# A dense first stage of seven-product blocks: two of its products made ahead for all chunks by a second level of seven products, through DRAM

## The chip, the cores and the metric

The kernel runs on one core of one Trainium2 chip. The metric is the device time of one execution in microseconds. A profile of one execution stands beside the times; its span runs from the first to the last instruction.

## The reference, cut to what matters

x has 2048 tokens of 640 numbers. The output mixes a Fourier layer and a dense layer with a gate per token:

```
g = sigmoid((x * gate_w).sum(-1))
a = x @ Wd_re.T ;  b = x @ Wd_im.T            # hidden transform, 640 x 640
y = Ws_re @ a - Ws_im @ b                      # sequence transform, 2048 x 2048
h = x @ w1 + b1                                # 640 -> 1728: the "dense first stage"
act = h * tanh(softplus(h))                    # Mish
out = g * y + (1 - g) * (act @ w2)             # 1728 -> 640
```

All in fp32, on the given drawn inputs.

## The kernel before, in words

**Precision.** TensorE works on fp32r. Each operand is split in a high and a low part (`split`, L84: ScalarE copies f to the high part, L82; VectorE subtracts it to make the low part, L79), and `mm3` (L93) makes three matmuls: high x high, high x low, low x high. A matmul has a 128 x 128 stationary weight block and 512 moving tokens. All matmuls are issued at L91.

**Stages.** Sequence transform, hidden transform, dense first stage, last stage, in this order. Tokens are moved in four groups of 512, t = 0 to 3, and a pair tp holds t1 = 2 tp and t2 = 2 tp + 1. Each stage does its matrix product with one level of a scheme of seven products in place of eight: the weights are seen as 2 x 2 blocks, so are the inputs, sums of blocks are multiplied, and the results are added up.

**The dense first stage** (`dense_first`, L766). w1 has 1728 columns: 13 chunks of 128 and a rest of 64. The first 12 chunks are worked as pairs f and f + 6 (six pairs, FP = 6), for each tp. x's 640 rows are five blocks of 128: 0 and 1 are the first half, 2 and 3 the second half, and the fifth one (d) is added as an ordinary product. The moving operands for one tp are a11, a12, a22 (blocks as they are), s1 to s4 (sums of blocks), and d1, d2; each but d has two blocks (k = 0, 1). The products of a pair of chunks are, in order: p1 (weights x a11, into bank a), p5 (x s1, bank b), d (x d2, bank d), p6 (x s2, added in bank a), p3 (x s4 and d1, bank b), p7 (x s3, bank a), p2 (x a12 and d1, bank c), p4 (x a22 and d2, bank a). p1 and p5 are copied out to SBUF by ScalarE (`snap`, L821) and added by VectorE to banks later (`add`, L828). Two chunk pairs are worked side by side, step by step. Mish is applied by ScalarE (`mish`, L703) and the result is stored to DRAM. Chunk 12 and the rest of 64 columns are done ahead of this, per t, in `dense_rest` (L705).

**x's sums.** In `sums_of` (L772) VectorE makes s1 to s4 from four loaded blocks of x, per tp and k, shortly before they are split.

**Weights.** `w1_job` (L637) makes the sums of w1's blocks and splits them: for each chunk pair three weight slots (a, b, c) and a part of a shared one (T2B).

**The order.** The program is written out as a list of steps; each step issues its matmuls. A planner (from L1060) walks the steps: it loads inputs up to AHEAD = 9 steps before they are prepared (L1076, on SP's queue), prepares a step's operands LEAD = 7 steps ahead (6 in the dense stage), issues stores some steps after the data is made (L1085, SP's queue), runs functions registered for a step (`at`), and then fills in background jobs (weight splits, gate rows, gated y rows) when its own clock of VectorE is behind its clock of TensorE. `need` forces a job that a step cannot do without. Buffers are pools handed out in turn: R (pairs rh, rl for moving operands, NR), FS (512 columns of fp32, NFS), FX (640 columns, NFX), W (weight pairs, NW). `lend` jobs turn a weight slot into an R pair (NL of them). No background jobs run in the steps of `quiet` (L1044).

Of the kernel before, what the change touches and what calls it, by code (L numbers as in the profile page):

```python
# [13 lines left out]
P = 128  # L14
N = 512
# [9 lines left out]
LEAD_D = 6  # L25
AHEAD = 9
SPARE, SPARE_D, SPARE_OUT = 3, 5, 4
SLACK, SLACK_UP = -1.0, 2.5
NR, NFS, NFX, NW, NL = 10, 20, 4, 26, 4
# [18 lines left out]
def fnet_mish_gate(ctx: ExitStack, tc: tile.TileContext, xn, xt, c_re, c_im, wd_re, wd_im,  # L48
# [78 lines left out]
    class Job:  # L127
        def __init__(self, key, work, load=lambda: [], w=0, fx=0, fs=0):
            self.key, self.work, self.load, self.w, self.fx, self.fs = key, work, load, w, fx, fs
# [498 lines left out]
    W1, W2C, T2B, extra = [None] * (FC + 1), {}, [None] * 2, []  # L628
# [7 lines left out]

    def w1_job(f, ga, gb):  # L637
        t = FS.get()
        a, b, c = W.get(), W.get(), W.get()
        if f % KD == 0:  # L640
            T2B[f // KD] = W.get()
# [8 lines left out]
        yield 1  # L650
        split(*part(b, 0, 2 * P), t[:, B2])
        split(*part(c, 0, 2 * P), ga[:, A2])
        yield 1
        split(*part(c, 2 * P, 4 * P), gb[:, A2])
        split(*part(c, 4 * P, 5 * P), t[:, :P])
        split(*part(T2B[f // KD], f % KD * P, f % KD * P + P), t[:, P:2 * P])
        FS.put(t)
        FX.put(ga, gb)
        W1[f] = (a, b, c)
# [24 lines left out]
    def dense_jobs():  # L684
        for _ in range(NL):
            jobs.append(Job("lend", simple(lend), w=1))
        jobs.append(Job("w1c", simple(w1c_job), lambda: [fx_load(w1a[FC - 1])], 1, 1))
        jobs.append(Job("w1r", simple(w1r_job), lambda: [fx_load(w1b, KD * FR)], 1, 1))
        for f in range(FP):
            jobs.append(Job(("w1", f), lambda a, b, f=f: w1_job(f, a, b),  # L690
                            lambda f=f: [fx_load(w1a[f]), fx_load(w1a[f + FP])], 3 + (f % KD == 0), 2))
# [13 lines left out]
    def dense_rest(t, keep, preps, end=False):  # L705
# [17 lines left out]
        def post_c():  # L723
            ps, a = H.pop("c"), FS.get()
            mish(a, ps, FC - 1)
            psum.put(ps)
            store(asc[FC - 1][t], a, a)
# [8 lines left out]
        def post_r():  # L736
# [7 lines left out]
            def then():  # L744
                nc.scalar.activation(a[q], a[q], AF.Mish)
                store(asc[FC][t], a[q], a)
            at(n + 2, then)
            if not keep:
                x_free(*keys)
            elif t % 2:  # L750
                x_free(*[("a21", k, t // 2) for k in range(2)])
# [9 lines left out]
        step(raw, [wait], mms_c, post_c)  # L761
        step([], [], mms_r, post_r)
        attach.append((preps[0], lambda: prep(0, 3)))
        attach.append((preps[1], lambda: prep(3, 5)))

    def dense_first(tp, end, ops):  # L766
# [3 lines left out]
        n0 = len(steps)  # L770

        def sums_of(k):  # L772
            raw = [(("xs", tp, a, k), xt[t, kk])
                   for a, t, kk in ((21, t2, k), (22, t2, k + 2), (11, t1, k), (12, t1, k + 2))]

            def prep():
                a21, a22, a11, a12 = (RAW.pop(r[0]) for r in raw)
                s1 = FS.get()
                tt(s1, a21, a22, OP.add)
                tt(a21, a11, a21, OP.subtract)  # L780
                tt(a22, s1, a11, OP.subtract)
                tt(a12, a12, a22, OP.subtract)
                FS.put(a11)
                XS[k] = {"s1": s1, "s2": a22, "s3": a21, "s4": a12}
            return raw, prep

        def make(name):
            def prep():
                if name[0] == "s":
                    for k in range(2):  # L790
                        x_split((name, k, tp), XS[k].pop(name))
                elif name[0] == "d":
# [6 lines left out]
        def sub(fp, ops, then=()):  # L799

            def mms():
                a, b, c = W1[fp]
                for bank, name, blk, start, stop in ops:
                    if start:
                        H[bank, fp] = psum.get()
                    for k in range(2):
                        mm3(H[bank, fp], *blk(a, b, c, k), *X[name, k, tp], start and k == 0, stop and k == 1)
                for bank, name, w, start, stop in then:
                    if start:
                        H[bank, fp] = psum.get()  # L810
                    mm3(H[bank, fp], *part((a, b)[w], 4 * P, 5 * P), *X[name, 0, tp], start, stop)
            return mms

        def at_cols(which, c0):
            return lambda a, b, c, k: part((a, b, c)[which], c0 + k * P, c0 + k * P + P)

        def t2_at(fp):
            return lambda a, b, c, k: part(c, 4 * P, 5 * P) if k == 0 else \
                part(T2B[fp // KD], fp % KD * P, fp % KD * P + P)
# [7 lines left out]

        def add(bank, name, fp, keep=False):  # L828
            f = KEEP[name, fp] if keep else KEEP.pop((name, fp))
            tt(f, H[bank, fp], f, OP.add)  # L830
            return f
# [12 lines left out]
        def parts(fp):  # L844
# [7 lines left out]
            def p1_post():  # L852
                snap("p1", "a", fp)
                free("a11")

            def p5_post():
                snap("p5", "b", fp)
                free("s1")

# [3 lines left out]

            def p3_post():
                o = add("b", "u2", fp)
# [4 lines left out]
            def p7_post():  # L870
                add("a", "p5", fp, True)
                free("s3")

            def p2_post():
                c11, c22 = add("c", "p1", fp), add("d", "p5", fp)
                pop("c", fp)
                pop("d", fp)
                i = clock["step"]
                at(i + 1, lambda: out_act(fa, t1, c11, c11))
                at(i + 2, lambda: out_act(fb, t2, c22, c22))  # L880
                free("a12", "d1")

            def p4_post():
# [7 lines left out]
                if end:  # L891
                    W.put(*W1[fp])
                    if fp in (KD - 1, FP - 1):
                        W.put(T2B[fp // KD])

            return [
                ([lambda: need(("w1", fp))], sub(fp, [("a", "a11", at_cols(0, 0), True, True)]), p1_post),
                ([], sub(fp, [("b", "s1", at_cols(2, 0), True, True)]), p5_post),
                ([], sub(fp, [], [("d", "d2", 1, True, True)]), None),
                ([], sub(fp, [("a", "s2", t2_at(fp), False, True)]), p6_post),  # L900
                ([], sub(fp, [("b", "s4", at_cols(1, 2 * P), False, False)], [("b", "d1", 1, False, True)]), p3_post),
                ([], sub(fp, [("a", "s3", at_cols(2, 2 * P), False, True)]), p7_post),
                ([], sub(fp, [("c", "a12", at_cols(0, 2 * P), True, False)], [("c", "d1", 0, False, True)]), p2_post),
                ([], sub(fp, [("a", "a22", at_cols(1, 0), False, False)], [("a", "d2", 0, False, True)]), p4_post)]


        for fp in range(0, FP, 2):
            for two in zip(parts(fp), parts(fp + 1)):
                for p in two:
                    step([], *p)  # L910
        for name, i in ops:
            if name[0] == "k":
                raw, prep = sums_of(int(name[1:]))
                steps[i][0].extend(raw)
                attach.append((i, prep))
                continue
            kk = {"a11": (t1, 0), "a12": (t1, 2), "a22": (t2, 2), "d1": (t1, 4), "d2": (t2, 4)}.get(name)
            if name[0] == "d":
                steps[i][0].append((("xd", tp, name), xt[kk]))
            elif kk:  # L920
                steps[i][0].extend((("xo", tp, name, k), xt[kk[0], kk[1] + k]) for k in range(2))
            attach.append((i, make(name)))
# [74 lines left out]
    for k in range(KS):  # L997
        jobs.append(Job(("gate", k), simple(lambda f, k=k: gate_rows(k, f)), lambda k=k: [x_rows(k)], fx=1 + (not k)))
    jobs.append(Job("mish", simple(lambda: nc.scalar.preload_act_table_set("mish"))))
# [27 lines left out]
    for tp in range(2):  # L1027
# [3 lines left out]
    dense_rest(2, False, (nd, nd))  # L1031
    dense_rest(3, False, (nd + 2, nd + 2))
    dense_rest(0, True, (nd + 6, nd + 8))
    dense_rest(1, True, (nd + 8, nd + 10), True)
    n0 = nd + 8
    dense_first(0, False, [("k0", n0 + 2), ("k1", n0 + 2), ("s1", n0 + 3), ("s2", n0 + 4), ("s4", n0 + 6), ("s3", n0 + 7)])
    n0 = len(steps)
    dense_first(1, True, [("a11", n0 - 8), ("k0", n0 - 4), ("k1", n0 - 3), ("s1", n0 - 2), ("d2", n0), ("s2", n0 + 2),
                          ("s4", n0 + 4), ("d1", n0 + 5), ("s3", n0 + 7), ("a12", n0 + 9), ("a22", n0 + 11)])
    for t in (2, 3):  # L1040
        at(n0 - 2, lambda t=t: QX.update({t: fx_load(qsc[t], N)}))
        at(len(steps) + 3, lambda t=t: FX.put(QX.pop(t)))
    narrow.update(range(nd, len(steps)))
    quiet = set(range(nd - 4, nd + 13))  # L1044
# [17 lines left out]
    unwritten = {id(d) for row in usc + asc for d in row}  # L1062
# [97 lines left out]
```

## Time and profile before

| what | value |
|---|---|
| median of the runs shown | 864.03 us (863.54 to 864.53, 2 runs) |
| the profiled execution | 864.04 us |
| its span | 862.3 us |
| TensorE / VectorE / ScalarE busy | 857.9 / 716.7 / 472.0 us |
| matmuls | 3775 |
| transfers | 214.12 MB, mean 248 GB/s |
| granted TensorE clock | 1.000 |

How to read the lines that follow: a row of a group gives the line, the engine, the operation, output<-input, the shape and the count, then busy us in all, mean ns of one, and the idle time of the engine just before them with what ended it. A row of a wait reads "who waited <- for whom: us in all, times, longest". A row of a stretch gives start:end, length, and then busy us and instruction count of TensorE, its weight loads, VectorE, ScalarE and GpSimd, then the granted clock, the share of transfer time in use and GB/s. The sequence stage ends near 396 us, the hidden stage near 519, the dense first stage near 689.

### The profile page before, as it was taken

How to read it: one execution, taken by the hardware profiler on the slowest of the kernel's cores; microseconds unless marked ns; L12 is line 12 of the kernel's file. 1: busy time of each engine (PE TensorE's matmuls, PEld its weight loads, DVE VectorE, ACT ScalarE, POOL GpSimd, SP SyncE). 2: the span in 40 equal slices, each digit the busy share in tenths (PEclk: the TensorE clock that was granted, in tenths of full speed). 3: DMA queues.
4: the chain of work that ended last, by engine and by line, in shares of the span. 5: the costliest groups of instructions: out<-in, count | busy, mean ns of one | idle time of the engine just before them, and what ended most of it. 6: DMA issues, size and time to landing. Idle time of an engine off the chain costs nothing.

```text
span 862.3 us, 12147 instructions
## 1 busy us (share of the span) xinstructions
PE 857.9 (99%) x3775; PEld 710.2 (82%) x3775; DVE 716.7 (83%) x1248; ACT 472.0 (55%) x883; POOL 0.2 (0%) x4
## 2 busy tenths in 40 slices
PE   9999999999999999999999999999999999999998
PEld 7888888888888888888888888888888888888886
DVE  6999987989869668998898896685677869999993
ACT  6756545454654545656667566654645647642442
POOL 0000000000000000000000000000000000000000
PEclk9999999999999999999999999999999999999999
DMA  9976748885868573778677697199784777894952
GB/s 348 323 240 221 245 158 303 299 277 200 287 225 280 175 252 119 248 269 302 234 251 241 238 336 252 56 306 334 252 297 165 254 240 237 281 346 169 357 203 109
DMA packets 116752, 214.12 MB, mean 248 GB/s; under 512 B 13520, under 2 KB 16080, under 8 KB 116688
## 3 DMA queue, kind: packets, MB, share of 16 engines
q1 hardware_dynamic: 116256, 212.71, 72.2%
q10 hardware_dynamic: 432, 0.66, 0.2%
q8 instruction: 29, 0.48, 0.2%
q14 instruction: 35, 0.29, 0.1%
HBM read 168.99 MB, written 44.32 MB: 247 GB/s over the span
## 4 chain that ended last, share of the span: by engine, by line
PE 99%; ACT 0%; issue 0%
PE ps L91 99%; ACT f L82 0%
## 5 line engine op out<-in xcount | busy, mean ns | idle before, releaser
L91 PE MATMUL ps<-rh,wh 128*128 128x512 f32 (+1 forms) x1083 | 420.3, 389 | 0.0
L91 PE MATMUL ps<-rh,wl 128*128 128x512 f32 x1067 | 414.1, 389 | 0.0
L91 PE MATMUL ps<-rl,wh 128*128 128x512 f32 x1061 | 411.9, 389 | 0.0
L82 ACT ACTIVATE rh<-f 128x512 fp32r<-128x512 f32 x416 | 245.9, 625 | 164.4 <-DVE f L79 105.8
L79 DVE TENSOR_TENSOR rl<-f,rh 128x512 fp32r<-128x512 f32 x414 | 269.7, 684 | 55.6 <-ACT rh L82 55.1
L91 PEld LDWEIGHTS ps<-rh,wh 128*128 128x128 f32 x1083 | 203.5, 188 | 42.4 <-ACT wh L82 0.2
L91 PEld LDWEIGHTS ps<-rh,wl 128*128 128x128 f32 x1067 | 200.3, 188 | 41.4
L91 PEld LDWEIGHTS ps<-rl,wh 128*128 128x128 f32 x1061 | 199.4, 188 | 41.3
L79 DVE TENSOR_TENSOR f<-f,f 128x512 f32<-128x512 f32 x309 | 210.9, 688 | 10.9 <-DMA f<-act 2.5
L82 ACT ACTIVATE f<-ps 128x512 f32<-128x512 f32 (+1 forms) x144 | 83.7, 596 | 86.7 <-PE ps L91 79.7
L82 ACT ACTIVATE wh<-f 128x512 fp32r<-128x512 f32 (+3 forms) x170 | 75.4, 482 | 57.8 <-DVE f L79 41.8
L79 DVE TENSOR_TENSOR wl<-f,wh 128x512 fp32r<-128x512 f32 (+3 forms) x170 | 81.2, 509 | 23.2 <-ACT wh L82 23.1
L79 DVE TENSOR_TENSOR f<-ps,f 128x512 f32<-128x512 f32 x89 | 57.6, 683 | 21.0 <-PE ps L91 20.9
L91 PE MATMUL ps<-wh,wh 128*128 128x512 f32 x187 | 72.7, 389 | 0.0
L91 PE MATMUL ps<-wl,wh 128*128 128x512 f32 x187 | 72.7, 389 | 0.0
L91 PE MATMUL ps<-wh,wl 128*128 128x512 f32 x181 | 70.4, 389 | 0.0
L703 ACT ACTIVATE f<-f,b1s 128x512 f32<-128x512 f32 x36 | 24.9, 719 | 41.5 <-DVE f L79 41.5
L91 PEld LDWEIGHTS ps<-wh,wh 128*128 128x128 f32 x187 | 35.1, 188 | 7.3
L91 PEld LDWEIGHTS ps<-wl,wh 128*128 128x128 f32 x187 | 35.1, 188 | 7.3
L91 PEld LDWEIGHTS ps<-wh,wl 128*128 128x128 f32 x181 | 34.0, 188 | 7.0
L79 DVE TENSOR_TENSOR wl<-fx,wh 128x640 fp32r<-128x640 f32 (+3 forms) x47 | 31.3, 679 | 3.6 <-ACT wh L82 3.6
L82 ACT ACTIVATE wh<-fx 128x640 fp32r<-128x640 f32 (+4 forms) x48 | 28.7, 612 | 7.9 <-DMA fx<-in_w1a_dram 4.4
(37 smaller groups left out, 162.7 us busy)
## 6 DMA issues: line engine op xcount, KB each, us to landing
f<-in_c_re_dram SPq DMA_DIRECT2D x128, 256.0 KB, 4.2
f<-in_c_im_dram SPq DMA_DIRECT2D x128, 256.0 KB, 4.3
f<-act SPq DMA_DIRECT2D x93, 256.0 KB, 5.4
f<-u SPq DMA_DIRECT2D x80, 256.0 KB, 4.6
act<-f SPq DMA_DIRECT2D x54, 256.0 KB, 4.0
f<-in_xt_dram SPq DMA_DIRECT2D x44, 256.0 KB, 4.9
u<-f SPq DMA_DIRECT2D x40, 256.0 KB, 3.3
y<-f SPq DMA_DIRECT2D x40, 256.0 KB, 4.6
```

The costliest lines, as they stand in the source:

```text
L79: nc.vector.tensor_tensor(o, a, b, op=op)
L82: nc.scalar.activation(o, a, AF.Copy, scale=scale)
L91: nc.tensor.matmul(ps, a, b, start=start, stop=stop, skip_group_check=True)
L703: nc.scalar.activation(o[rows], src[rows], AF.Mish, bias=b1s[rows, f:f + 1])
```

## The change

1. *Products p1 and p5 for all chunks at once.* For all twelve chunks and both token pairs p1 is one product of a block of w1 (6 chunks x 2 k) with x's a11 (2 k x 2 tp). It is itself cut in 2 x 2 blocks: chunk 2g and 2g + 1, k = 0 and 1, tp = 0 and 1, and made with seven products for each of three groups g (`dense_quads`). p5 is done likewise with the sums s1. The results are stored to DRAM, and in `dense_first` they are loaded again (`part_load`, 12 steps ahead for p1, 9 for p5) and copied by ScalarE into the banks a, b, c, d before the other products are added there (`seed`). Two of p5's results stay in SBUF.
2. *Weights for it*: three `quad_job`s of three weight slots each, held to the end of the prelude. `w1_job` splits less.
3. *The order*: the seven-product steps (q) and the eight steps of `dense_rest` (r) are interleaved as "rqqrqqrqqrq", once for p1, once for p5.
4. *x's sums made early* (`x_sum_jobs`): background jobs behind the gate rows load blocks of x, VectorE makes the sums, and they are stored to DRAM; later they are loaded like inputs, 6 steps ahead.
5. *The main part* has six products for a pair of chunks instead of eight. d's result is copied out to SBUF and added in p7's step; p2's Mish reads its bank directly.
6. *Sizes*: NR 10 to 8, NFS 20 to 24, NL 4 to 6 (two of them lent early), SPARE_D 5 to 2, `quiet` from 17 steps to 8; activations of `dense_rest` are stored one step after they are made instead of three.

The diff, cut to its core:

```
-SPARE, SPARE_D, SPARE_OUT = 3, 5, 4
-NR, NFS, NFX, NW, NL = 10, 20, 4, 26, 4
+LEAD_P = 12
+R_LOAD, X_LOAD = 6, 6
+SPARE, SPARE_D, SPARE_OUT = 3, 2, 4
+SLACK, SLACK_UP, SLACK_D = -1.0, 2.5, 1.0
+NR, NFS, NFX, NW, NL = 8, 24, 4, 26, 6
...
+    def quad_job(g, l, m):
+        t = FS.get()
+        wa, wb, wc = QW[g] = W.get(), W.get(), W.get()
+        tt(m, m, l, OP.subtract)
+        def sums(l, t):
+            v = l.rearrange("p (a b) -> p a b", b=P)
+            tt(t[:, A2].rearrange("p (a b) -> p a b", b=P), v[:, 2:4], v[:, 0:3:2], OP.subtract)
+            tt(t[:, 2 * P:3 * P], l[:, 3 * P:], t[:, :P], OP.subtract)
+            tt(t[:, 3 * P:], l[:, P:2 * P], t[:, 2 * P:3 * P], OP.subtract)
+        sums(l, t)
+        yield 1
+        split(*part(wc, 0, 2 * P), l[:, A2])
+        split(*part(wa, 4 * P, 5 * P), l[:, 3 * P:])
+        split(*part(wa, 0, 4 * P), t)
...
     def w1_job(f, ga, gb):
-        split(*a, ga)
+        split(*part(a, 0, 3 * P), ga[:, 2 * P:])
...
+    def x_sum_jobs():
+        def pair(tp, *fs):
+            for k in range(2):
+                f, g = fs[2 * k:2 * k + 2]
+                tt(f, f, g, OP.add)
+                FS.put(g)
+                store(XQ["p5", "a" + "12"[tp] + "12"[k]], f, f)
+        def quad(n, a11, a12, a21, a22):
...
+        def main(tp, k, a21, a22, a11, a12):
...
+        def add(key, work, srcs):
+            jobs.append(Job(key, simple(work), lambda: [fs_load(v) for v in srcs], fs=5))
...
+    def dense_quads(name):
...
+        for b, x, w, post in (("b", "a12", "b21", lambda: snap("b", "q2")), ("a", "a11", "b11", lambda: add("a", "q2", 0, 0)),
+                              ("b", "s1", "t1", lambda: snap("b", "q5")), ("a", "s2", "t2", lambda: snap("a", "u2")),
+                              ("b", "s4", "b22", c12), ("a", "s3", "t3", lambda: add("a", "q5", 1, 1)),
+                              ("a", "a22", "t4", out)):
+            def mms(b=b, x=x, w=w):
+                start = x in ("a12", "a11", "s1")
+                for g, v in enumerate(bank):
+                    if b not in v:
+                        v[b] = psum.get()
+                    mm3(v[b], *block(g, w), *X[name, x], start, True)
...
+            load_at(len(steps) - X_LOAD, [((name, x), XQ[name, x])])
+            at(len(steps) - 3, lambda x=x: x_split((name, x), RAW.pop((name, x))))
...
+        def seed(bank, name, fp, last=False):
+            f = RAW[name, fp, tp]
+            H[bank, fp] = psum.get()
+            copy(H[bank, fp], f)
...
-                ([lambda: need(("w1", fp))], sub(fp, [("a", "a11", at_cols(0, 0), True, True)]), p1_post),
-                ([], sub(fp, [("b", "s1", at_cols(2, 0), True, True)]), p5_post),
-                ([], sub(fp, [], [("d", "d2", 1, True, True)]), None),
-                ([], sub(fp, [("a", "s2", t2_at(fp), False, True)]), p6_post),
...
+                ([], sub(fp, [("a", "s2", at_cols(0, 3 * P), False, True)]), p6_post),
+                ([], sub_d(fp), d_post),
...
+                at(n + j - LEAD_P, lambda f=f: part_load("p1", f))
+                if tp or fp:
+                    at(n + j - LEAD_P + 3, lambda f=f: part_load("p5", f))
+                at(n + j - 5, lambda f=f: seed("a", "p1", f))
+                at(n + j - 1, lambda f=f: (seed("b", "p5", f), seed("d", "p5", f, True)))
+                at(n + j + 3, lambda f=f: seed("c", "p1", f, True))
...
+    rests = [s for t in (2, 3, 0, 1) for s in [dense_rest(t, t < 2, t == 1)] * 2]
+    for name in ("p1", "p5"):
+        quads = dense_quads(name)
+        for o in "rqqrqqrqqrq":
+            next(quads if o == "q" else rests.pop(0))
...
-    quiet = set(range(nd - 4, nd + 13))
+    quiet = set(range(nd - 4, nd + 4))
```

More of the change, by code (lines that the diff above doesn't have):

```diff
@@ L703, in mish, with take, load_at, load @@
         nc.scalar.activation(o[rows], src[rows], AF.Mish, bias=b1s[rows, f:f + 1])
-    def dense_rest(t, keep, preps, end=False):
+    def take(i, n):
+        takes[i] = takes.get(i, 0) + n
+    def load_at(i, raw):
+        def load():
+            assert not any(id(src) in unwritten for _, src in raw)
+            RAW.update({key: fs_load(src) for key, src in raw})
+        take(i, len(raw))
+        at(i, load)
+    def dense_rest(t, keep, end):
         names, five = (("a21", "a22"), "d2") if t % 2 else (("a11", "a12"), "d1")
@@ L1102, in fnet_mish_gate @@
                 FS.put(FX.get()[:, :N])
[L1103 removed]
+        while clock["dve"] < clock["pe"] + (SLACK_D if i in narrow else SLACK if ("seq", "low", KH - 1) in done_jobs else SLACK_UP) and i >= wait_until and i not in quiet:
             if running:
```

270 lines of the change are left out of this document (171 added, 99 removed).

## The prediction, made before the result was known

> **What bounds the kernel now.** I read the page's shares and its chain, then the chain in order of time, the waits of TensorE, and the table of stretches.
>
> ```profile
> span 862.3 us, 12147 instructions
> PE 857.9 (99%) x3775; PEld 710.2 (82%) x3775; DVE 716.7 (83%) x1248; ACT 472.0 (55%) x883; POOL 0.2 (0%) x4
> PE ps L91 99%; ACT f L82 0%
> ```
> ```profile
> 0.77 857.93 PE ps L91 x3775
> ```
> ```profile
> PE ps L91 <- PEq L1148: 0.8, 1, 0.8
> ```
> ```profile
> 20.00:840.00 820.00, 820.00 (x3620) 679.20 (x3619) 695.09 (x1211) 453.23 (x850) 0.00 (x0) 1.00 0.73 250
> 230.00:340.00 110.00, 110.00 (x487) 91.13 (x486) 81.87 (x132) 55.82 (x98) 0.00 (x0) 1.00 0.66 220
> 380.00:519.00 139.00, 139.00 (x615) 115.11 (x614) 126.33 (x225) 89.28 (x175) 0.00 (x0) 1.00 0.75 259
> 519.00:689.00 170.00, 170.00 (x752) 140.81 (x751) 121.66 (x223) 97.03 (x184) 0.00 (x0) 1.00 0.71 240
> ```
>
> TensorE's matmuls are one unbroken chain: 857.93 us in one piece, and the only wait in its list is the 0.8 us before the first. A busy matmul row alone would prove little, since matmuls overlap; the pace does. In the 820 us from 20 to 840 it starts 3,620 matmuls, 820/3620 = 0.2265 us each, at granted clock 1.00 (the column behind POOL), and the dense stage (519 to 689) has the same pace: 170/752 = 0.226. My count from the code is 3,775 (9 warm-ups, 1,730 sequence stage, 540 hidden stage, 748 dense stage, 748 last stage), equal to the page's, so no record is missing. Time is therefore number of matmuls times 0.2265 us, as long as nothing comes late; nothing does now, so no wait can be won back. The profiled execution took 864.04 us, 1.74 outside its span, and the median of the runs is 864.03: the sum below is made against 864.04.
>
> **The change part by part: matmuls.** In the dense first stage each pair of chunks (six pairs, two halves of the tokens) has now p1 6, p5 6, d 3, p6 6, p3 9, p7 6, p2 9, p4 9 = 54 matmuls; 54 x 12 = 648. Without p1 and p5 it is 42; 42 x 12 = 504. The prelude makes these two products with seven block products for three groups, 3 matmuls each: 2 x 7 x 3 x 3 = 126, where they cost 144 before. Net -18 matmuls, 3,757 left: -18 x 0.2265 = -4.08 us. That is all the change can win, because only TensorE is on the path: 864.04 - 4.08 = 859.96.
>
> **What is added beside TensorE.** Rows for the prices:
>
> ```profile
> L79 DVE TENSOR_TENSOR rl<-f,rh 128x512 fp32r<-128x512 f32 x414 | 269.7, 684 | 55.6 <-ACT rh L82 55.1
> L82 ACT ACTIVATE rh<-f 128x512 fp32r<-128x512 f32 x413 | 244.3, 625 | 164.4 <-DVE f L79 105.8 <-PE ps L91 43.5 <-DMA f<-act 7.9
> L79 DVE TENSOR_TENSOR f<-f,f 128x512 f32<-128x512 f32 x307 | 209.7, 688 | 10.9 <-DMA f<-act 2.5 <-DMA y<-f 2.3 <-DMA out_dram<-f 0.5
> L82 ACT ACTIVATE f<-ps 128x512 f32<-128x512 f32 x140 | 81.3, 596 | 83.0 <-PE ps L91 76.1 <-DVE rl L79 1.6 <-DMA act<-f 1.3
> L79 DVE TENSOR_TENSOR f<-ps,f 128x512 f32<-128x512 f32 x89 | 57.6, 683 | 21.0 <-PE ps L91 20.9
> L82 ACT ACTIVATE ps<-f 128x512 f32<-128x512 f32 x26 | 14.5, 595 | 8.7 <-DVE fx L79 8.1 <-DVE f L79 0.6
> L79 DVE TENSOR_TENSOR wl<-fx,wh 128x640 fp32r<-128x640 f32 x28 | 22.8, 818 | 2.2 <-ACT wh L82 2.2
> L79 DVE TENSOR_TENSOR wl<-f,wh 128x128 fp32r<-128x128 f32 x51 | 12.4, 283 | 0.0
> L79 DVE TENSOR_TENSOR wl<-f,wh 128x256 fp32r<-128x256 f32 x26 | 10.9, 418 | 4.9 <-ACT wh L82 4.9
> ```
> ```profile
> 515.94 3.08 DVE L79 TENSOR_TENSOR rl<-f,rh 128x512 fp32r<-128x512 f32 x5
> ```
>
> Columns: busy us, mean ns of one, idle time before. In a row of five, VectorE starts one each (3.08 - 0.68)/4 = 0.60 us, so 0.60 is what one of 512 columns takes of its time.
>
> *x's sums, made early.* 24 adds, 24 x 0.60 = 14.4 us of VectorE, queued behind the gate rows, in place of 16 adds in the dense stage. From 230 to 340 VectorE is idle 110 - 81.9 = 28.1 us and these jobs need no weight slots, so I cost them at nothing. They carry 32 loads and 24 stores of 0.262 MB = 14.7 MB; at share 0.66 there are 37 us of transfer time free, at 220/0.66 = 333 GB/s room for 12.5 MB, so they reach past 340. Without that cover VectorE's 14.4 us fall on the hidden stage (second rival).
>
> *Weights.* The three quad jobs: each one add of 512, two of 256 and four of 128, two splits each of 512, 256 and 128; on VectorE 0.69 + 2 x 0.42 + 4 x 0.28 + 2 x (0.68 + 0.42 + 0.28) = 5.4 us, 16.2 for three, before the first prelude product. The other weight jobs split 384, 384 and three times 256 instead of 640, 384, three of 256 and two of 128: about 0.8 us less each (0.82 + 2 x 0.28, less a second 384, which I estimate between the 256 and 640 rows at 0.55). VectorE is idle 139 - 126.3 = 12.7 us from 380 to 519; the lateness this can cause lies between 0 and 16.2 - 12.7 = 3.5 us if every gap is used, 16.2 if none is. I take 0.6: steps are prepared six or seven ahead (about 9 us at 6 matmuls each), and most of the weight jobs of the six pairs move behind the prelude.
>
> *Prelude, 226 matmuls = 51.2 us.* ScalarE gets 24 copies out (14.3 us at 0.596) and 14 more splits (8.8) beside the 20 splits and eight Mish calls it has; VectorE 18 adds (12.3 at 0.683) and 14 splits (9.6). Neither fills 51 us. One place is tight: product a22 goes on in the banks that three adds of s3 still read. Three adds take 3 x 0.60 = 1.8 us, a split ahead of them 0.6, and the only step between is 10 matmuls = 2.27 us. So 0.1 to 0.5 us each, in both sequences: I take 0.3 x 2 = 0.6. The end below: 0; above: 2 us each if a weight job gets in front.
>
> *Main part.* Per pair and half, ScalarE gains four seed copies into banks (4 x 0.595) and one copy out (d) and loses two (p1, p5): +1.8 us, 21 over all, on 55% use. VectorE loses two adds of four, 12 x 2 x 0.68 = 16 us. TensorE waits for a seed; the tightest is d's second, copied behind one copy out and one other seed (about 3 x 0.5 us at back-to-back pace, an estimate from the 0.595 row) with 1.36 + 0.68 = 2.04 us of matmuls to hide it. I take 0; it can cost 0 to 0.5 us for each of six pairs if a weight split gets between, up to 3 us.
>
> *Slots.* Eight pairs of rh/rl instead of ten are just the seven steps prepared ahead and the one in use. I take 0 (bounds 0 to 2): seven steps of six matmuls are 7 x 6 x 0.2265 = 9.5 us, and ScalarE's rh row, with 43.5 us of waiting for TensorE, shows that it already runs as far ahead as the pairs let it.
>
> **Sum.** 859.96 + 0.6 (VectorE at the seam) + 0.6 (banks) = **861.2 us**.
>
> **Transfers: the first rival (slower than before).**
>
> ```profile
> DMA packets 22202, 40.78 MB, mean 239 GB/s; under 512 B 2513, under 2 KB 3281, under 8 KB 22190
> f<-in_xt_dram SPq DMA_DIRECT2D x23, 256.0 KB, 5.0
> fx<-in_w1a_dram SPq DMA_DIRECT2D x4, 320.0 KB, 3.0
> ```
> ```profile
> 360.00:380.00 20.00, 20.00 (x90) 16.57 (x89) 19.66 (x32) 8.46 (x15) 0.00 (x0) 1.00 1.02 362
> 580.00:600.00 20.00, 20.00 (x90) 16.57 (x89) 9.93 (x16) 8.46 (x14) 0.00 (x0) 1.00 0.96 344
> 800.00:820.00 20.00, 20.00 (x90) 16.54 (x90) 18.72 (x31) 10.53 (x20) 0.00 (x0) 1.00 1.05 366
> ```
> ```profile
> 541.00:561.00 20.00, 20.00 (x90) 16.57 (x89) 13.31 (x31) 13.07 (x29) 0.00 (x0) 1.00 0.21 64
> ```
> ```profile
> SPq L1085 <- DVE f L79: 100.3, 58, 21.9
> ACT wh L82 <- DMA f<-act: 9.4, 2, 5.7
> ```
>
> The first rows are the transfers from 519 to 690: 40.8 MB. Added there: 22 stores and 22 loads of partial products, 44 x 0.262 = 11.5 MB; x loads 43 of 52 instead of 23, +5.2 MB; weight pairs that now load later, about +2.0. That is 59.5 MB in 730 x 0.2265 = 165.3 us, or 360 GB/s, as much as the two fullest stretches of 20 us moved (362, 366). At the 344 of the third row it takes 173 us, 7.7 more: 867.7. It decides from where the stage sustains less than 59.5/(165.3 + 4.1) = 351 GB/s: then the time is above 864. For it: SP's queue is one line, and a store that waits for VectorE holds the loads behind it (100.3 us of such waits, the longest 21.9), x's loads now stand only six steps ahead of their split, and ScalarE already waits up to 5.7 us for a transfer at 690. Against it: partial products load 12 steps ahead, the gated y rows and last-stage weights are not urgent, and the stretch 541 to 561 is nearly empty now (64 GB/s). Time 867.7, chance 0.22.
>
> The Trainium skill, "DMA: Bandwidth & Descriptors", section Specifications, gives about 358 GB/s from HBM for a core; by that figure, as an estimate, the stage's transfers take 166 us and cost 1 us. "HBM Reference", section Specifications (TRN2), says that a core streaming alone gets about 425, by which they cost nothing. The trace has 362 and 366 over 20 us, past the first and short of the second.
>
> **Second rival: VectorE at the seam.** x's sums slip past 340 and with the quads make 14.4 + 16.2 = 30.6 us; only 28.1 + 12.7 = 40.8 us are idle from 230 to 340 and from 380 to 519, many of them gaps behind copies. A third of the work finding no gap, 10 us, less some 5 us of lead, leaves 5: with the 0.6 of the banks 865.6. For it: 126 of 139 us busy; against: it catches up at once after 519 (122 of 170). Chance 0.17.
>
> **Third rival: starved jobs, over 2%.** Each sums job needs five free buffers beyond the spare ones and stands ahead of the hidden stage's weights. If loads of the sequence stage keep the pool low, those weight jobs are forced at their use, one load after another.
>
> ```profile
> f<-in_wd_re_dram SPq DMA_DIRECT2D x5, 256.0 KB, 4.6
> fx<-in_wd_im_dram SPq DMA_DIRECT2D x5, 320.0 KB, 4.8
> ```
>
> Five such waits of 4.7 us are 23 us: 884. For it: the buffers are the only guard; against: there are 24 of them, not 20. Chance 0.08.
>
> A fourth: the waits just eat the gain and it stays at 864, chance 0.06; it lies between the others.
>
> **How the numbers follow.** Forecast (859.6 to 863) 0.47, transfers 0.22, seam 0.17, starved 0.08, even 0.06. Below 859.6 nothing leads: the matmuls left need 859.96, and runs differ by half a us. The range 859.6 to 868.5 leaves out the starved case and the worst of the transfers, 0.14 together; the forecast's own range is 859.6 to 863. 2% is 17.3 us, about what a measurement of this kernel tells from no change: 18 matmuls cannot give that, and only the starved case, or transfers below 320 GB/s, take it: faster 0.01, within 0.90, slower 0.09.
>
> **What would show it.** After: 3,757 matmuls, pace 0.2265 elsewhere; no new row in TensorE's waits of over 1 us, VectorE about 735 us busy (716.7 - 16.4 for the adds + 8 more adds and 8 more splits of x 11.0 + quads 16.2 - 5.0 for the other weights + 12.3 in the prelude = 734.8). Wrong by transfers: dense stage above 0.95 DMA share with waits of ScalarE or VectorE on loads there. Wrong at the seam: TensorE waiting on rl or wl near 515 to 530. Wrong by starving: waits on wh before 420.

## The result, and the profile after

The changed kernel takes 887.34 us (median; 886.42 to 888.26) against 864.03 before: 1.027 times as long, 95% interval 1.0217 to 1.0322. It is slower, outside the range of the prediction, and 26.1 us above its 861.2. The profiled execution took 888.26 us. These are its page's lines, then the two longest pieces of its chain of waits, then TensorE's waits (columns as before). The chain of waits goes from the last instruction back, at each step, to what released it; a row of it gives the start, the length in us, and what stood there.

```profile
span 886.5 us, 12425 instructions
PE 863.4 (97%) x3757; PEld 707.0 (80%) x3757; DVE 736.5 (83%) x1285; ACT 517.5 (58%) x957; POOL 0.2 (0%) x4
PE 75%; DMA 11%; DVE 6%; ACT 5%; issue 2%; SPq 1%; DVEq 0%; ACTq 0%
```
```profile
0.77 226.58 PE ps L94 x989
...
269.93 264.40 PE ps L94 x1165
```
```profile
PE ps L94 <- ACT ps L85: 8.8, 5, 5.6
PE ps L94 <- DVE f L82: 5.0, 5, 1.5
PE ps L94 <- DVE rl L82: 2.2, 4, 0.8
PE ps L94 <- ACT f L85: 1.1, 1, 1.1
```

The 3,757 matmuls are there, 18 fewer, and VectorE's 736.5 us are the forecast's 735. But the one unbroken chain of before is cut: TensorE is 75% of it, transfers 11%. TensorE's busy share hides this (97%): a matmul's row lasts 0.39 us at a pace of 0.2265, so rows overlap and a late start leaves little idle time between them. What counts is how many matmuls a stretch starts. The same three stretches before and after, and for after the two between and behind them:

```profile
230.00:290.00 60.00, 60.00 (x266) 49.73 (x265) 49.53 (x78) 31.49 (x55) 0.00 (x0) 1.00 0.72 237
520.00:600.00 80.00, 80.00 (x355) 66.26 (x354) 53.61 (x102) 46.56 (x92) 0.00 (x0) 1.00 0.68 232
600.00:740.00 140.00, 140.00 (x620) 115.95 (x619) 109.55 (x198) 77.09 (x148) 0.00 (x0) 1.00 0.74 248
```
```profile
230.00:290.00 60.00, 58.51 (x257) 47.76 (x256) 52.64 (x84) 27.55 (x49) 0.00 (x0) 1.00 0.97 344
290.00:520.00 230.00, 230.00 (x1016) 190.53 (x1015) 207.47 (x364) 138.86 (x259) 0.00 (x0) 1.00 0.74 259
520.00:600.00 80.00, 72.42 (x305) 56.01 (x304) 58.77 (x111) 60.19 (x120) 0.00 (x0) 1.00 0.88 309
600.00:740.00 140.00, 130.40 (x555) 105.08 (x554) 87.94 (x163) 93.47 (x179) 0.00 (x0) 0.98 0.87 309
740.00:850.00 110.00, 110.00 (x487) 91.10 (x486) 103.77 (x166) 54.04 (x96) 0.00 (x0) 1.00 0.80 275
```

Matmuls missing against before, times 0.2265 us: 9 or 2.0 us from 230 to 290 (where x's sums are made), 50 or 11.3 us from 520 to 600 (the prelude), 65 or 14.7 us from 600 to 740 (the main part): 28.1 us lost. From 290 to 520 and from 740 on the pace is full. Less the 4.1 us won that is 24.0 us; the two profiled executions lie 24.2 apart, the medians 23.3.

*What stands at 540 to 600.* The weight splits of the six pairs of chunks on VectorE (count: shortest/median/longest ns, first and last start, shapes), before and after; ScalarE's half of them in after up to 567; ScalarE in order of time (start, us, engine, line, operation, shapes, count, and in brackets the idle time before it and what ended it); then two pieces of after's chain of waits.

```profile
L79 DVE TENSOR_TENSOR wl<-fx,wh x21: 412/426/826, 457.1 to 574.0; 128x256 fp32r<-128x256 f32 x11, 128x640 fp32r<-128x640 f32 x5, 128x384 fp32r<-128x384 f32 x5
```
```profile
L82 DVE TENSOR_TENSOR wl<-fx,wh x18: 417/551/562, 540.1 to 604.2; 128x384 fp32r<-128x384 f32 x12, 128x256 fp32r<-128x256 f32 x6
```
```profile
L85 ACT ACTIVATE wh<-fx x8: 403/514/532, 539.3 to 558.8; 128x384 fp32r<-128x384 f32 x6, 128x256 fp32r<-128x256 f32 x2
```
```profile
539.30 0.95 ACT L85 ACTIVATE wh<-fx 128x384 fp32r<-128x384 f32 x2
540.13 0.69 ACT L745 ACTIVATE f<-ps,b1s 128x512 f32<-128x512 f32 x1
540.70 0.64 ACT L85 ACTIVATE rh<-f 128x512 fp32r<-128x512 f32 x1
542.24 0.88 ACT L85 ACTIVATE wh<-f 128x256 fp32r<-128x256 f32 x2 [0.90 <-DVE f L82]
```
```profile
559.21 5.02 DMA act<-f
564.25 5.68 DMA f<-p5s
```

In after all six weight jobs run between 540 and 604, in and right behind the prelude, whose last partial product is stored at 580; half of their twelve splits of 384 columns start by 559 on ScalarE. The 542.24 row shows how that hurts: ScalarE idles 0.90 us for sums that VectorE is still making for the weight split, and every copy out, x split and seed queued behind that split waits with it. Nothing is full on average (VectorE 58.8 and ScalarE 60.2 of 80 us). From 560 to 580, where 19 of the 50 matmuls are missing, the chain goes through transfers as well: a store (act<-f), then the load of an x sum (f<-p5s).

*What stands at 600 to 640.* The chain of waits of after; the loads of gated y rows before and after (count: shortest/median/longest ns of issuing one, first and last start); the DMA issues from 580 to 640 (the last number is the median us to landing); VectorE's wait on loads from 600 to 640; and two stretches of 20 us:

```profile
600.20 4.56 DMA f<-y
...
604.82 5.82 DMA f<-p
610.66 5.26 DMA f<-y
...
622.23 6.39 DMA act<-f
628.69 4.99 DMA act<-f
```
```profile
L145 SPq DMA_DIRECT2D f<-y x20: 376/440/1132, 561.5 to 634.8; - x20
```
```profile
L148 SPq DMA_DIRECT2D f<-y x20: 320/426/919, 591.7 to 626.1; - x20
```
```profile
f<-y SPq DMA_DIRECT2D x20, 256.0 KB, 5.4
y<-f SPq DMA_DIRECT2D x18, 256.0 KB, 5.2
act<-f SPq DMA_DIRECT2D x14, 256.0 KB, 5.8
```
```profile
DVE f L82 <- DMA f<-y: 11.3, 5, 4.7
```
```profile
600.00:620.00 20.00, 20.00 (x89) 16.32 (x88) 15.06 (x27) 14.15 (x27) 0.00 (x0) 1.00 1.05 397
620.00:640.00 20.00, 14.44 (x51) 11.33 (x51) 5.69 (x9) 7.24 (x13) 0.00 (x0) 0.83 1.00 364
```

All twenty gated y rows (load, product with g, store; 44 transfers with the four rows of g) are issued from 591 to 643. Their loads took 73 us before and take 34 now. From 600 to 640 the transfers run at share 1.00 to 1.05, each takes 5 to 6 us, and both engines are half idle. VectorE, which takes its work in order, stands 11.3 us before products whose row hasn't landed. ScalarE and TensorE in order of time show the end of it:

```profile
622.25 0.69 ACT L745 ACTIVATE f<-ps,b1s 128x512 f32<-128x512 f32 x1 [4.25 <-DMA y<-f]
...
630.02 0.60 ACT L85 ACTIVATE f<-ps 128x512 f32<-128x512 f32 x1 [4.92 <-DMA act<-f]
630.51 1.11 ACT L85 ACTIVATE ps<-f 128x512 f32<-128x512 f32 x2
```
```profile
625.73 0.39 PE L94 MATMUL ps<-rh,wl 128*128 128x512 f32 x1
631.67 0.79 PE L94 MATMUL ps<-rh,wh 128*128 128x512 f32 x1 [5.56 <-ACT ps L85]
...
637.39 0.53 PE L94 MATMUL ps<-wl,wh 128*128 128x512 f32 x1
637.75 0.39 PE L94 MATMUL ps<-wh,wl 128*128 128x512 f32 x1
```

ScalarE waits 4.25 and 4.92 us not for data but for a place to write: the buffer it was handed is still being stored (y<-f, act<-f). Behind the copy out at 630.02 stand the seeds (ps<-f), and behind those TensorE, 5.56 us. Then the 13 matmuls from 631.67 to 637.39 take 0.44 us each (5.72/13), not 0.2265: 2.8 us more, at a lower clock (0.83 is the mean granted from 620 to 640).

### The profile page after: what moved, and what is told of

Its sections match the earlier page's. It is cut to its first block, busy times and chain, and to the rows that moved or that the text cites. A ratio compares the mean times of both kernels' runs of the same rounds, so it can differ in the third digit from the quotient of the medians.

```text
span 886.5 us, 12425 instructions
## 1 busy us (share of the span) xinstructions
PE 863.4 (97%) x3757; PEld 707.0 (80%) x3757; DVE 736.5 (83%) x1285; ACT 517.5 (58%) x957; POOL 0.2 (0%) x4
## 4 chain that ended last, share of the span: by engine, by line
PE 75%; DMA 11%; DVE 6%; ACT 5%; issue 2%; SPq 1%; DVEq 0%; ACTq 0%
PE ps L94 75%; DMA act<-f 4%; DVE f L82 3%; DVE rl L82 2%; ACT wh L85 2%; DMA y<-f 1%; ACT f L85 1%; DMA f<-y 1%; DVE wl L82 1%; ACT rh L85 1%; ACT ps L85 1%; DMA f<-in_xt_dram 1%; ACT f L745 1%; DMA f<-p 1%; DMA f<-xs 1%
## 5 line engine op out<-in xcount | busy, mean ns | idle before, releaser
L94 PE MATMUL ps<-rh,wl 128*128 128x512 f32 x1051 | 408.4, 390 | 0.0
L85 ACT ACTIVATE rh<-f 128x512 fp32r<-128x512 f32 x420 | 255.3, 628 | 211.4 <-PE ps L94 95.7
L82 DVE TENSOR_TENSOR rl<-f,rh 128x512 fp32r<-128x512 f32 x420 | 275.1, 687 | 50.9 <-ACT rh L85 49.6
L82 DVE TENSOR_TENSOR f<-f,f 128x512 f32<-128x512 f32 (+2 forms) x332 | 221.4, 675 | 28.1 <-DMA f<-y 11.3
L85 ACT ACTIVATE f<-ps 128x512 f32<-128x512 f32 (+1 forms) x157 | 89.5, 595 | 52.4 <-PE ps L94 35.2
L85 ACT ACTIVATE wh<-f 128x512 fp32r<-128x512 f32 (+3 forms) x182 | 82.4, 488 | 56.3 <-DVE f L82 45.7
L82 DVE TENSOR_TENSOR wl<-f,wh 128x512 fp32r<-128x512 f32 (+3 forms) x182 | 88.7, 519 | 28.3 <-ACT wh L85 27.9
L94 PE MATMUL ps<-wh,wh 128*128 128x512 f32 x198 | 78.8, 398 | 5.8 <-DVE f L82 3.7
L82 DVE TENSOR_TENSOR f<-ps,f 128x512 f32<-128x512 f32 x83 | 53.6, 684 | 12.6 <-PE ps L94 12.5
L85 ACT ACTIVATE ps<-f 128x512 f32<-128x512 f32 x76 | 43.2, 593 | 10.8 <-DVE f L82 10.8
L82 DVE TENSOR_TENSOR f<-fx,f 128x256 f32<-128x256 f32 (+1 forms) x70 | 29.9, 450 | 1.7
```

Of the source, the lines that this page charges most:

```text
L82: nc.vector.tensor_tensor(o, a, b, op=op)
L85: nc.scalar.activation(o, a, AF.Copy, scale=scale)
L94: nc.tensor.matmul(ps, a, b, start=start, stop=stop, skip_group_check=True)
```

## The experiments

Theories, by the letters of the expectations: A, the bytes of the partial products overload the transfers (the prediction's first rival); B, the weight jobs' work in the prelude; C, SP's one line of loads and stores; D, the burst of gated rows. In the sixth, ninth and later runs the parts are combined. The kernel before took 863.57 to 863.96 beside them. Ratios are to it, with 95% intervals; the last columns are matmuls started in the three stretches (266, 355 and 620 before; 257, 305 and 555 after; one missing is 0.2265 us).

| run | us | ratio | 230-290 | 520-600 | 600-740 |
|---|---|---|---|---|---|
| 1 partial products narrow | 883.46 | 1.0227 (1.0194 to 1.0260) | 258 | 317 | 554 |
| 2 no weight work | 877.31 | 1.0156 (1.0127 to 1.0186) | 259 | 339 | 565 |
| 3 both | 874.05 | 1.0118 (1.0088 to 1.0149) | 258 | 350 | 564 |
| 4 stores on GpSimd's queue | 882.06 | 1.0211 (1.0181 to 1.0241) | 256 | 311 | 574 |
| 5 no gated rows | 876.19 | 1.0147 (1.0118 to 1.0177) | 259 | 304 | 606 |
| 6 = 2 + 5 | 867.81 | 1.0056 (1.0036 to 1.0076) | 257 | 344 | 608 |
| 7 gated rows paced | 878.56 | 1.0174 (1.0145 to 1.0204) | 257 | 305 | 597 |
| 8 five spare buffers | 881.15 | 1.0205 (1.0175 to 1.0234) | 260 | 304 | 580 |
| 9 weight work on GpSimd | 885.05 | 1.0245 (1.0198 to 1.0292) | 260 | 331 | 545 |
| 10 = 7 + 9, x sums paced | 871.00 | 1.0083 (1.0053 to 1.0112) | 261 | 334 | 597 |
| 11 = 10, loads eight ahead | 869.37 | 1.0068 (1.0053 to 1.0083) | 260 | 331 | 613 |
| 12 = 11, last weights on GpSimd | 880.22 | 1.0193 (1.0176 to 1.0210) | 259 | 329 | 582 |
| 13 = 6, no x sums | 865.31 | 1.0019 (1.0010 to 1.0029) | 266 | 341 | 608 |
| 14 = 13, loads eight ahead | 866.98 | 1.0042 (1.0025 to 1.0059) | 267 | 340 | 607 |
| 15 = 11, weights in place | 876.31 | 1.0152 (1.0137 to 1.0167) | 250 | 308 | 602 |
| 16 = 15, weights spread | 877.26 | 1.0163 (1.0148 to 1.0178) | 258 | 331 | 578 |

**1 to 3: bytes, weights, both.** Run 1 stores and loads only 128 of the 512 columns of each partial product (three quarters of the partial products are left out). Run 2 leaves out the six weight jobs' splits and sums, with buffers, slots and the planner's count of their time as they were. Run 3 does both.

```
-            RAW[name, f, tp] = fs_load(qout[name][f][tp])
+            RAW[name, f, tp] = FS.get()
+            nc.sync.dma_start(RAW[name, f, tp][:, :P], qout[name][f][tp][:, :P])
...
-            nc.sync.dma_start(dst, v)
+            nc.sync.dma_start(dst[:, :P], v[:, :P])
```
```
     def w1_job(f, ga, gb):
...
-        split(*part(a, 0, 3 * P), ga[:, 2 * P:])
-        split(*part(b, 2 * P, 5 * P), gb[:, 2 * P:])
+        clock["dve"] += 2 * (0.14 + 0.54 * 384 / N)
...
```

> Changed kernel with the stores and loads of the partial products cut from 512 to 128 columns: same transfers, waits and order, 8.6 MB less in the dense stage (60.8 to 52 MB); it leaves three quarters of the partial products out. Theory A (the transfers of the dense stage are saturated from 600 to 660, and late landings hold ScalarE, which holds TensorE): the 14 to 17 us of TensorE time lost behind 600 shrink to under 6, time 872 to 877. Theory B (weight jobs stand ahead of copies and seeds in ScalarE's and VectorE's line in the prelude): no more than 3 us, 884 to 888.

> Changed kernel whose six weight jobs of the chunk pairs keep their loads, slots and place in the plan but issue none of their 30 splits and 24 sums (leaves the dense stage's weight splits out). Theory B: the 10 us that TensorE loses from 540 to 600 go, time 876 to 879, and the stretch 600 to 660 stays as it is. Theory A: the loss from 540 to 600 shrinks by less than 4 us, time 883 to 887.

> Both edits of the first two runs at once. If A and B together are the cause, nearly all of the 28 us go: 861 to 867. If a third cause holds (the landing time of each transfer and not its bytes, or SP's one line of loads and stores), 870 or more stays.

Run 1 gained 3.9 us, between the two theories' figures, and none of it from 600 to 740 (554), where most of the partial products are loaded. A falls as the main cause. Run 2 gained 10.0 us, in the prelude:

```profile
520.00:600.00 80.00, 78.23 (x339) 62.97 (x338) 48.08 (x76) 57.83 (x106) 0.00 (x0) 1.00 1.00 352
```

34 matmuls more than after, 7.7 us, though more bytes moved in the stretch (352 GB/s against 309): B holds, and the engines are the larger part of what the prelude runs short of. The bytes of the partial products are a smaller one: narrow, they give the prelude 12 matmuls alone (run 1 against after) and 11 beside run 2's edit (run 3 against run 2), 2.7 and 2.5 us. With both edits its chain of waits has 232 matmuls in one piece:

```profile
519.80 52.62 PE ps L94 x232
```

Both together gave 874.05 where 861 to 867 was expected: a miss, and the 600 to 740 stretch (564) says that something else stands there.

**4 and 5: SP's line, the gated rows.** Run 4 issues the stores of the dense stage from GpSimd's queue, so that no store holds up a load. Run 5 keeps the gated rows' buffers but neither loads, multiplies nor stores (the gating of y is left out).

```
-            nc.sync.dma_start(dst, v)
+            (nc.gpsimd if i in narrow else nc.sync).dma_start(dst, v)
```
```
-                                lambda t=t, d=d: ([fs_load(gsc[t])] if d == 0 else []) + [fs_load(ysc[d][t])], fs=2))
+                                lambda t=t, d=d: ([FS.get()] if d == 0 else []) + [FS.get()], fs=2))
...
-        tt(y, y, GT[t], OP.mult)
-        store(ysc[d][t], y, y)
+        clock["dve"] += 0.14 + 0.54
+        store(None, y, y)
```

> Changed kernel with all stores of the dense stage issued by GpSimd's queue, so that no load stands behind a store that waits. Theory C (SP's one line): the loads come earlier, time 870 to 880. Theory A: the same bytes move at the same time, 884 to 892.

> Changed kernel whose 20 gated-row jobs keep their buffers and places in the plan but issue no load, product or store (44 transfers of 256 KB and 20 products are left out, so y stays ungated). Theory D (these jobs are packed into some 40 us behind the weight jobs, and copies out of banks then land in buffers whose stores are still under way): the loss from 610 to 660 goes, 871 to 876. Theory A (bytes of the partial products) has been cut down by the first run to 4 us; if the loss is inherent in the six-product part (copies, seeds and adds in one line), 882 or more stays.

Run 4 gained 5.3 us, between what C and A asked for: the line is a part, not the main cause. Run 5 gained 11.2 us, and most of the loss of the main part is gone, 51 of 65 matmuls or 11.6 us:

```profile
600.00:740.00 140.00, 138.19 (x606) 113.11 (x605) 88.26 (x164) 100.69 (x193) 0.00 (x0) 1.00 0.78 263
```

**6 to 8: both causes out; the burst alone.** Run 6 is runs 2 and 5 together. Runs 7 and 8 compute all of the output: run 7 loads gated rows at least two steps apart, run 8 raises the buffers that a job leaves spare from two to the five of before.

```
-        while jobs and len(loaded) < (6 if i in narrow else 2) ...
+        while jobs and not (jobs[0].key[0] == "yg" and i < last_yg + 2) and len(loaded) < (6 if i in narrow else 2) ...
+            last_yg = i if jobs[0].key[0] == "yg" else last_yg
             job_load(i)
```
```
-SPARE, SPARE_D, SPARE_OUT = 3, 2, 4
+SPARE, SPARE_D, SPARE_OUT = 3, 5, 4
```

> Changed kernel without the gated rows' transfers and products and without the splits and sums of the six weight jobs (both left out, plan unchanged). Theories B and D together: 862 to 866, little above the 860 that the matmuls alone give. If the seeds or the banks cost by themselves: 868 or more.

> Changed kernel with one line in the planner: a gated-row job is loaded no sooner than two steps after the one before. Nothing is left out. Theory D: the burst spreads over more time, 874 to 881; if the transfers' mean rate and not their burst holds the kernel, 884 to 889.

> Changed kernel with the number of buffers that background jobs leave free in the dense stage put back from 2 to 5 (SPARE_D). Theory D, with the lack of free buffers as its core: fewer gated rows under way at once, copies wait less for stores, 874 to 882. If the buffers are not the point: 884 to 889.

Run 6 lands 1.8 us above its range: 19.5 of the 27.4 us above 859.96 are these two (10.0 and 11.2 alone, so they share 1.7). Run 7 is the sharpest of all: the same rows, the same bytes, one condition in the planner, and 8.8 us come back. Its loads of gated rows, and its stretch:

```profile
L148 SPq DMA_DIRECT2D f<-y x20: 319/427/1142, 591.4 to 660.2; - x20
```
```profile
600.00:740.00 140.00, 136.21 (x597) 111.10 (x596) 94.03 (x173) 98.12 (x189) 0.00 (x0) 1.00 0.91 322
```

The loads take 69 us as against 34, more is moved (322 GB/s against 309), and 42 more matmuls start. So it is the bunching, not the amount. Run 8 gets 6.2 us, with 25 more matmuls from 600 to 740: the change's own cut of SPARE_D from five to two is a part of this loss.

**9 to 12: attempts to keep the change and mend it.** All four compute the whole output. Run 9 gives the splits and sums of the six weight jobs to GpSimd; run 10 adds run 7's pacing and loads x's sums' inputs at least five steps apart; run 11 loads x blocks eight steps ahead, not six; run 12 gives the last stage's weight splits to GpSimd as well.

```
+    def ptt(o, a, b, op):
+        clock["dve"] += 0.14 + 0.54 * a.shape[-1] / N
+        nc.gpsimd.tensor_tensor(o, a, b, op=op)
+    def psplit(h, l, src):
+        nc.gpsimd.tensor_copy(h, src)
+        ptt(l, src, f32(h), OP.subtract)
     def w1_job(f, ga, gb):
...
-        split(*part(a, 0, 3 * P), ga[:, 2 * P:])
+        psplit(*part(a, 0, 3 * P), ga[:, 2 * P:])
...
+        while jobs and not (jobs[0].srcs and i < last_x + 5) and ...
...
-R_LOAD, X_LOAD = 6, 6
+R_LOAD, X_LOAD = 8, 8
...
-        split(*part(w, 0, 3 * P), a)
+        (psplit if st.kind == "out" else split)(*part(w, 0, 3 * P), a)
```

> Changed kernel with the splits and sums of the six weight jobs moved whole to GpSimd, which is idle; nothing is left out. Theory B (they stand in ScalarE's and VectorE's line ahead of the prelude's copies): most of the 10 us lost from 540 to 600 go, 877 to 881. If what counted in the second run was that the weights themselves came late, GpSimd being slower makes it worse: 886 or more.

> Changed kernel with three edits, nothing left out: weight jobs on GpSimd, gated rows loaded at least two steps apart, x-sum jobs loaded at least five steps apart. If the three places are independent: 887.3 less 10, 9 and 1.5 us, 865 to 869. If they share one cause, or GpSimd is too slow to keep the gated rows behind it on time: 870 or more.

> The kernel with all three edits, and the loads of x for the prelude and the main part 8 steps ahead of their use instead of 6; nothing left out. If the 3.7 us still lost from 560 to 580 come from a load issued 5.5 us before its split (a wait of 5.5 us for f<-p5s ends there): they go, 867 to 868.5. If it is the copies of the prelude in one line on ScalarE: no change, 870 to 872.

> As the run before, and the splits of the last stage's weights (made in the dense stage's second half) on GpSimd too; nothing left out. Theory B holds there as well (the weight splits stand ahead of seeds and adds from 660 to 700, 3.5 us): 863 to 866. If GpSimd delivers them too late: TensorE waits at the start of the last stage, 870 or more.

Run 9 missed: the prelude gains 26 matmuls, and the burst behind it then costs ten more than in after, so the whole gains only 2.3 us. Each loss hides a part of the other's mending. Run 10 is 2 us above its first range, in its second case. Run 11 is between its two cases, and its gain does not lie in the prelude, where the first put it (334 to 331), but behind it (597 to 613). Run 12 is in its second case: from 680 to 700 it starts 61 matmuls, where run 11 starts 89, and GpSimd's splits of the last stage's weights are in the chain of waits from 670 to 690. Run 11, 869.37, is the best complete version, and it is still slower than before.

**13 to 16: the rest, and the weights again.** Run 13 is run 6 with x's sums left out as well (empty jobs; plain blocks of x are loaded in the sums' place); run 14 adds the longer lead. Run 15 is run 11 with the weight jobs back on ScalarE and VectorE, run 16 the same with the four parts of a weight job two steps apart; 15 and 16 compute the whole output.

```
-            jobs.append(Job(key, simple(work), lambda: [fs_load(v) for v in srcs], fs=5))
+            jobs.append(Job(key, simple(work), lambda: [FS.get() for v in srcs], fs=5))
...
     def w1_job(f, ga, gb):
...
-        yield 1
+        yield 2
```

> The kernel of the sixth experiment (no gated rows, no weight work of the six pairs) with the x-sum jobs also empty: they take and return their buffers, and count in the planner's clock, but load, add and store nothing, and the later loads read plain blocks of x of the same size in place of the sums (leaves out the sums of x). 867.81 without this. Theory X: these jobs' loads ahead of the sequence stage's own cost the 1.7 us lost from 230 to 290 and nothing else: 865.5 to 866.6, and that stretch full. Rival: the smaller pools (8 pairs) cost it there: 867 to 868.5. If they cost more than that stretch, in the prelude too: below 865.

> The kernel just before, and the loads of x blocks and partial products issued eight steps ahead of their use in place of six. Theory: the 2.5 us still lost from 560 to 580 are one late load of x's sums for the prelude (the chain shows a 5.7 us transfer there), so 862.5 to 864.5. Rival: the load is late because no buffer is free or because what it waits for is late, and two steps more of lead change nothing: within 0.5 us of the kernel before it.

> Complete kernel: gated rows at least two steps apart, x-sum loads at least five apart, loads eight ahead, and the weight jobs where they were, on ScalarE and VectorE. Against it the eleventh run had them on GpSimd, 869.37. If GpSimd relieves the prelude as the second experiment's kernel without weight work suggests: 874 to 877 here, with 9 to 11 us lost from 520 to 600. Rival: GpSimd's slowing of VectorE took most of its gain back: 868 to 872.

> The kernel just before, and the four parts of each weight job at least two steps apart where they were one. Theory: the loss from 520 to 600 comes of weight parts that follow one another without room for the prelude's copies, so spread they fit: 866 to 869. Rival: the prelude has not the room for them at all, so they are forced later at their use: no better than the kernel before, 874 to 878.

Run 13, its stretches and the chain of waits at the prelude:

```profile
230.00:290.00 60.00, 60.00 (x266) 49.67 (x265) 48.96 (x77) 31.29 (x52) 0.00 (x0) 1.00 0.72 237
520.00:600.00 80.00, 78.69 (x341) 63.27 (x340) 39.59 (x63) 57.23 (x105) 0.00 (x0) 1.00 0.88 314
600.00:740.00 140.00, 138.17 (x608) 113.30 (x607) 94.16 (x171) 97.49 (x185) 0.00 (x0) 1.00 0.79 268
```
```profile
539.14 5.93 DMA p<-f
...
545.98 6.02 DMA f<-in_xt_dram
```

x's sums cost 2.5 us (867.81 to 865.31, 0.2 below the expected range), and without them that stretch is full. In after VectorE waits there 3.6 us for a load of x (to 244.6) and 2.5 us for the store of a sum (to 249.3), and is then 98% busy up to 290; TensorE's two waits, 0.7 and 0.8 us, are on VectorE. Run 13 leaves out loads, sums and stores at once, so which of them decides is not shown; loading the inputs five steps apart (run 10) changed the stretch by one matmul against run 9. Of what is left, 14 matmuls (3.2 us) are missing in the prelude and 12 (2.7 us) in the main part. In the prelude a load stands behind a store (p<-f) in the chain; the longer lead did not mend it (run 14: in neither of its cases, 1.7 us above run 13 though the intervals meet, and one matmul fewer in the prelude). Run 3 bears on it: with narrow partial products only 5 are missing there, against 16 in run 2, which points to their bytes for most of this rest; that edit was not tried on run 13's kernel. Whether a load waits for its buffer, still being stored, or is slowed by the stores beside it was not tried. In the main part the chain of run 13 goes from ScalarE to VectorE and back from 632 to 654, copies out, seeds and Mish; which of them can't be spared stays open. Run 15 is where its first case said: GpSimd saves 6.9 us of the weights' cost. Run 16, in its rival's range (877.26), shows bunching and want of room at once: spread, the weights give the prelude 23 matmuls back (5.2 us) and take 24 from the main part, where they come later.

## Why the prediction was wrong, by its own steps

- **Count of matmuls, -4.08 us, and VectorE's total: right**, 3,757 and 736.5 us. The pace is 0.2265 in every undisturbed stretch.
- **Prelude, "Neither fills 51 us", with "most of the weight jobs of the six pairs move behind the prelude", costed at nothing: the first failed step, 10.0 us** (run 2). The sum of work was right and was the wrong measure. Half of the weight jobs fell in the prelude (VectorE's splits from 540 to 573) and half right behind it (582 to 604), ahead of copies out, x splits and seeds on engines that work in order. Before, weights were split there too, up to 574, with no loss (355 matmuls): there nothing of the prelude stood behind them. Beside TensorE's time the planner counts VectorE's alone, so ScalarE's share of each split is free to it; which engine's share cost more was not separated.
- **"The gated y rows ... are not urgent": the second, 11.2 us** (run 5). They aren't urgent, but nothing in the queue knows it. They were ready to load all at once behind the weight jobs, and their 44 transfers and 20 products took the transfers, the buffers and VectorE's place in line from work that is. The prediction gave no price to SPARE_D, five to two, which let more of them in (run 8: 6.2 us).
- **x's sums, "I cost them at nothing": 2.5 us** (run 13). VectorE had the idle time named, but not when it was needed: from 240 to 250, busy 3.75 of 10 us, it stood before a load and a store, and had no room left behind them. The transfers, at share 0.97 there as against 0.72 before, had been counted (14.7 MB into room for 12.5) and let pass.
- **Seam 0.6: near 0.** 1,016 matmuls from 290 to 520 is the full pace; the second rival falls, and no wait of TensorE for a weight stands before 519, so the third falls too.
- **Banks 0.6, slots and seeds 0: not told apart.** They lie, with the bytes of the partial products in the prelude (2.5 us, run 3 against run 2), in the 5.35 us that run 13 has left above 859.96, where the forecast allowed 1.2.
- **The transfers as a rival: the right place by another mechanism.** 59.5 MB were forecast, and after's row from 520 to 713 has 315 GB/s for 193 us, 60.8; what it expected to see, share near 1 and waits on transfers, stands at 600 to 640. But runs 1 and 7 show that neither the added bytes nor the mean rate decide: three quarters of the partial products fewer gave 3.9 us, the same bytes spread out 8.8. The waits are on stores, for the buffer, as much as on loads: from 600 to 640 ScalarE waits 16.7 us on stores and VectorE 11.3 on loads. A mean rate over 165 us could not show that, and the price of this rival, 7.7 us, lies below the 11.2 of run 5.

Taken out together, the three named costs are 22.0 us (887.34 to 865.31) of 27.4.

## What to carry to other kernels

Where one engine runs without a gap, an added stage is not to be costed by whether the busy sums fit: list, for the 20 us around it, what else will stand in each in-order line ahead of its copies, and where displaced background work comes to lie. Ask of each background job what keeps it from coming all at once, in transfers and buffers as in engine time. And a buffer is free only when its store has landed, 5 to 6 us later when transfers are full.

## What the runs showed of the hardware

**VectorE beside GpSimd.** From 540 to 600, VectorE's rows in after, then in run 11, where GpSimd splits weights:

```profile
L82 DVE TENSOR_TENSOR f<-ps,f 128x512 f32<-128x512 f32 x19 | 12.1, 684 | 0.0
L82 DVE TENSOR_TENSOR rl<-f,rh 128x512 fp32r<-128x512 f32 x15 | 10.0, 683 | 6.4 <-ACT rh L85 6.4
```
```profile
L82 DVE TENSOR_TENSOR rl<-f,rh 128x512 fp32r<-128x512 f32 x14 | 14.7, 1066 | 3.5 <-ACT rh L85 3.4
L82 DVE TENSOR_TENSOR f<-ps,f 128x512 f32<-128x512 f32 x18 | 11.5, 680 | 2.0 <-PE ps L94 2.0
```

With both inputs in SBUF the same instruction took 1066 ns in place of 683; with one in PSUM it stayed at 680. That is a price of moving work to GpSimd that the expectations of runs 9 to 12 left out. The Trainium skill, "SBUF — State Buffer", section "Who interferes with whom", says just this of a VectorE instruction with two SBUF inputs, and the rows agree.

**The clock after a stall.** A wait of 5.56 us was followed by 13 matmuls of 0.44 us, 2.8 us more, so this stall cost half as much again as it lasted. The Trainium skill, "TensorE: Matmul & The Clock Gate", Part 1, halves the clock after an idle window of some 3.4 us; the rows agree.

**Transfers.** The stretch from 600 to 620 moved 397 GB/s, past the 362 and 366 of the prediction's fullest rows.
